# A new order for the first five units of a linear-attention stage, own-key weights by matrix products, and a bank moved

## The chip, the cores and the metric

The kernel runs on one core of one Trainium2 chip. The metric is the device time of one execution in microseconds: the median of three runs is 386.19 us (385.58 to 386.66). The engines are named as in the profile: PE (TensorE, matrix products), PEld (its weight loads), DVE (VectorE), ACT (ScalarE), POOL (GpSimd) and SP, which issues the DMAs. TensorE's granted clock is 1.00 at 2.4 GHz and 0.50 at 1.2 GHz.

## The reference

Three stages follow each other. The first is a linear attention with a decaying state, for 4 batches, 8 heads, 768 steps and head size 48:

```python
for t in range(S):
    kt, vt, rt = (k[:, :, t], v[:, :, t], r[:, :, t])
    cur = np.einsum('bhd,bhe->bhde', u[None] * kt, vt)
    y[:, :, t] = np.einsum('bhd,bhde->bhe', rt, state + cur)
    state = w[None, :, :, None] * state + np.einsum('bhd,bhe->bhde', kt, vt)
```

The weight of a step's own key is therefore sum over d of r * u * k, and that of an earlier step is r * k times a power of w. The second stage is a soft mixture of 8 experts with 4 slots each: logits x @ phi, one softmax over the 3072 tokens and one over the 32 slots, w1 (384 to 1024), a relu and w2 back. The third is a feed-forward layer: 384 to 2048, the square of the relu, 2048 to 384.

## The kernel before

A *unit* is a pair of heads of one batch: 16 units of 768 steps, cut into six chunks of 128 (three even, three odd). For a unit these steps are issued, each by a small function of its own:

- `load_unit`: one row per partition with r in its natural layout, r turned (heads by steps), k turned and v in its natural layout; 1344 KB, in five buffers. It is issued on SP's queue.
- `decay(n, m)`: DVE multiplies turned r (m = 0) or turned k (m = 1) by powers of w, held in a PSUM table `tabp` that DVE builds first.
- `turns(x, k)`: PE transposes unit k's keys back, in chunks of 48 columns, and, where x is given, the output of unit x. ACT copies both out.
- `A(n, par)`: PE forms the 128 by 128 score blocks of the even or odd chunks, in two tiles of the tag `ps("A")`, which has three banks.
- `pr1(n)`, `pr2(n)`, `weigh(n)`: POOL multiplies natural r by u and the inverse decay and then by the keys, and DVE sums over d. That gives `dg`, the own-key weights.
- `diag(n, par)`: POOL writes `dg` on the diagonal of an otherwise zero block `AT`. `cp(n, par)`: DVE copies the scores below the diagonal into it (copy_predicated, one instruction per head).
- `KV(n)`, `scan(n)`: PE forms the six chunk states, DVE runs the recurrence over them. `inter(n)` and `intra(n, par)`: PE forms the outputs from the states and from the blocks; ACT copies them out to `xT`. `L(n)`: PE adds the logits.

Each engine takes its instructions in the order in which the program issues them, and that order is written by hand: a prologue (L463 to L494) starts units 0 to 2, and a loop over n then interleaves unit n's last steps with the first ones of n+1, n+2 and n+3. After the last step of unit n the loop issues the load of unit n+5 and pieces of the expert weights. In the loop turn with n % 4 == 1 `both` (L389) transposes the exponentials and the logits of the batch that has just been finished, into the bank of tag `lg`, in which the next batch's logits will be summed; in turn 2 DVE also builds two small tables, `sel` and `rm` (L512, L514).

Ahead of the prologue `keep_clock(7)` issues seven products of the identity matrix with itself.

Of the kernel before, what the change touches and what calls it, by code (L numbers as in the profile page):

```python
# [17 lines left out]
def rwkv_softmoe_ffn(ctx: ExitStack, tc: tile.TileContext, un, k0, wt, u, phi, w1, w2, w_in, w_out, out):  # L18
    nc = tc.nc
    NU, NPC, _, PW = un.shape  # L20
    H, D = u.shape
    NP = H // 2
    B = NU // NP
    DM, NTOK = out.shape
    S = NTOK // B
# [5 lines left out]
    NS = phi.shape[1]  # L31
# [4 lines left out]
    NQ = 4  # L36

# [75 lines left out]
    k0n = kns[0]  # L113
    load_unit(0, (nc.sync, nc.sync, nc.sync))
    nc.scalar.dma_start(k0n.rearrange("p c h d -> p (c h d)"), k0)
    nc.scalar.dma_start(U0.rearrange("p b d -> p (b d)"),
                        u.rearrange("(a b) d -> a (b d)", b=2)[0:1].rearrange("a x -> (a x)").partition_broadcast(128))
    load_unit(1)
    phs = att.tile([112, NP, 2, NS], F32, name="phs")
    ident = const.tile([128, 128], F32, name="ident")  # L120
    make_identity(nc, ident)
    nc.gpsimd.memset(phs, 0.0)
    for hh in range(2):
        for par in range(2):
            nc.sync.dma_start(phs[64 * (hh ^ par):64 * (hh ^ par) + D, :, par],
                              phi.rearrange("(a b d) s -> b d a s", b=2, d=D)[hh])
# [79 lines left out]
    cur = pw[:, 0]  # L206
    nc.vector.memset(tabp[:, :, 64:65], 1.0)
    nc.vector.reciprocal(cur[:, :, 0], base[:, :NP])
    nc.vector.tensor_copy(cur[:, :, 1], base[:, :NP])
    nc.vector.tensor_copy(tabp[:, :, 63:64], cur[:, :, 0:1])  # L210
    for i in range(6):
        n = 1 << i
        blk = tabp[:, :, 64 - 2 * n:64 + 2 * n].rearrange("p a (q x) -> p a q x", q=4)
        nc.vector.tensor_tensor(blk[:, :, 0::3], blk[:, :, 1:3], cur.unsqueeze(3).to_broadcast([112, NP, 2, n]), ALU.mult)
        nxt_ = pw[:, (i + 1) % 2]
        nc.vector.tensor_mul(nxt_[:, :, 1], cur[:, :, 1], cur[:, :, 1])
        if i < 5:
            nc.vector.reciprocal(nxt_[:, :, 0], nxt_[:, :, 1])
        cur = nxt_

    def keep_clock(n):
        if n:
            p = ps("A")
        for _ in range(n):
            nc.tensor.matmul(p[:, :256], ident, ident.unsqueeze(1).to_broadcast([128, 2, 128]), start=True, stop=True)
# [20 lines left out]
    def turns(x, k):  # L246
# [142 lines left out]
    def both(b):  # L389
        p = ps("lg")[:, :384].rearrange("p (k h g) -> p k h g", k=2, h=2)  # L390
# [79 lines left out]
    nc.vector.tensor_tensor(rsc, tabp, uw.unsqueeze(2).to_broadcast([112, NP, 128]), ALU.mult)  # L470
    decay(0, 1, EV)
    decay(0, 0, EV)
    A(0, 0)
    decay(0, 1, OD)
    pp = ps("lg")
    for a in range(NP):
        nc.tensor.transpose(pp[:, a * 128:a * 128 + 112], rsc[:, a], ident[:112, :112])
    nc.scalar.copy(UT, heads(pp.rearrange("p (a e) -> p a e", a=NP)))  # L478
    turns(None, 0)
    weigh(0)  # L480
    diag(0, 0)
    decay(0, 0, OD)
    diag(0, 1)
    pr1(1)
    decay(1, 1)
    cp(0, 0)
    KV(0)
    turns(None, 1)
    pr2(1)
    decay(2, 1)  # L490
    scan(0)
    decay(1, 0)
    for x in xn:
        nc.gpsimd.memset(x[:, :, DM:DM + 1], 1.0)  # L494
# [3 lines left out]
    for _ in range(3):  # L498
        i, c = pieces.pop(0)
        load_weight(i, (c,))  # L500
    NL = NU - NB
    for j, pc in enumerate(pieces):
        loads[j * (NL + 3) // len(pieces)].append(pc)
    for n in range(NU):
# [5 lines left out]
        if n == 2:  # L510
# [56 lines left out]
        if n + NB < NU:  # L567
            load_unit(n + NB)
        for i, c in loads[n]:
            load_weight(i, (c,))  # L570
# [360 lines left out]
def _layout(r, k, v, w, u, w2):  # L931
# [15 lines left out]
    row = np.concatenate([nat(r), turned(r), turned(k), nat(v)], axis=2)  # L947
# [7 lines left out]
    return un, nat(k)[0], wt, u, w2p  # L955
# [27 lines left out]
```

## Time and profile before

| what | number |
|---|---|
| median of three runs | 386.19 us |
| the profiled execution's own time | 386.27 us |
| its span, first to last instruction | 384.5 us |
| PE busy | 370.6 us, 96% of the span |
| DVE busy | 270.2 us, 70% |
| ACT, POOL busy | 204.6 us, 104.8 us |
| mean granted TensorE clock | 0.978 |
| chain that ended last | PE 88%, DMA 4%, DVE 4% |

The profiled execution takes 1.8 us more than its span, and is 0.08 us above the median. PE's busy share hides that its first 28 us differ from the rest, so the profile is read by stretches: the attention stage ends at about 122 us, the experts at about 155 us, and the feed-forward layer fills the rest.

### The profile page before, as it was taken

How to read it: one execution, taken by the hardware profiler on the slowest of the kernel's cores; microseconds unless marked ns; L12 is line 12 of the kernel's file. 1: busy time of each engine (PE TensorE's matmuls, PEld its weight loads, DVE VectorE, ACT ScalarE, POOL GpSimd, SP SyncE). 2: the span in 40 equal slices, each digit the busy share in tenths (PEclk: the TensorE clock that was granted, in tenths of full speed). 3: DMA queues.
4: the chain of work that ended last, by engine and by line, in shares of the span. 5: the costliest groups of instructions: out<-in, count | busy, mean ns of one | idle time of the engine just before them, and what ended most of it. 6: DMA issues, size and time to landing. Idle time of an engine off the chain costs nothing.

```text
span 384.5 us, 8703 instructions
## 1 busy us (share of the span) xinstructions
PE 370.6 (96%) x3537; PEld 300.0 (78%) x3537; DVE 270.2 (70%) x470; ACT 204.6 (53%) x436; POOL 104.8 (27%) x115
## 2 busy tenths in 40 slices
PE   6799999999999999999999999999999999999996
PEld 4678988887878654788787888888888888888884
DVE  5669888989963387599886677566656675666563
ACT  2223444454444233599787866555555665555553
POOL 4566767777741322133222220000000000000000
PEclk9559999999999999999999999999999999999999
DMA  6979998998999999614242104000000030000004
GB/s 232 388 313 375 339 367 283 390 322 306 406 388 358 406 418 370 237 52 122 86 120 72 41 2 164 1 2 0 0 2 0 27 139 0 1 2 0 0 2 165
DMA packets 23176, 66.29 MB, mean 172 GB/s; under 512 B 3296, under 2 KB 4832, under 8 KB 23136
## 3 DMA queue, kind: packets, MB, share of 16 engines
q1 hardware_dynamic: 22848, 65.38, 45.7%
q8 instruction: 28, 0.46, 0.5%
q10 hardware_dynamic: 288, 0.34, 0.3%
q14 instruction: 12, 0.10, 0.1%
HBM read 60.21 MB, written 4.72 MB: 169 GB/s over the span
## 4 chain that ended last, share of the span: by engine, by line
PE 88%; DMA 4%; DVE 4%; ACT 2%; issue 1%; ACTq 0%; DVEq 0%
PE ps_A L915 26%; PE ps_Y L915 9%; PE ps_kv L915 9%; PE ps_lg L915 8%; PE ps_A L304 6%; PE ps_tr L820 6%; PE ps_YO L334 3%; PE ps_A L635 3%; PE ps_YE L343 3%; PE ps_Y L656 3%; PE ps_YO L343 3%; DMA slot<-in_un_dram 3%; PE ps_kv L316 2%; PE ps_lg L357 2%; DMA slot<-in_u_dram 2%; PE ps_YE L268 1%
## 5 line engine op out<-in xcount | busy, mean ns | idle before, releaser
L844 DVE TENSOR_TENSOR slot<-slot,slot 128x512 fp32r<-128x512 f32 (+1 forms) x97 | 71.8, 741 | 53.6 <-PE ps_kv L915 18.5
L915 PE MATMUL ps_A<-slot,slot 128*128 128x512 f32 x432 | 105.8, 389 | 0.0
L915 PEld LDWEIGHTS ps_A<-slot,slot 128*128 128x128 f32 x432 | 81.0, 188 | 17.1 <-ACT slot L841 0.3
L841 ACT CAST slot<-slot 128x512 fp32r<-128x512 f32 (+1 forms) x97 | 59.7, 616 | 49.5 <-DVE slot L838 49.2
L831 ACT ACTIVATE slot<-ps_tr 128x512 f32<-128x512 f32 (+1 forms) x97 | 57.4, 593 | 23.2 <-PE ps_tr L820 22.3
L838 DVE TENSOR_TENSOR slot<-slot 128x512 f32<-128x512 f32 (+1 forms) x71 | 48.4, 684 | 11.5 <-ACT slot L831 11.2
L915 PE MATMUL ps_Y<-slot,slot 128*128 128x512 f32 x144 | 55.4, 391 | 0.0
L915 PE MATMUL ps_kv<-slot,slot 128*128 128x512 f32 x144 | 55.1, 389 | 0.0
L915 PE MATMUL ps_lg<-slot,slot 128*128 128x512 f32 x144 | 55.0, 389 | 0.0
L309 DVE COPY_PREDICATED AT<-mask,ps_A 128x384 f32<-128x384 int32 x64 | 34.0, 586 | 12.3 <-PE ps_A L304 4.2
L304 PE MATMUL ps_A<-slot 48*128 48x128 f32 x384 | 35.2, 303 | 4.6 <-DVE slot L235 3.2
L820 PE MATMUL ps_tr<-slot,slot 128*128 128x512 f32 x96 | 37.4, 391 | 0.4 <-DVE slot L784 0.4
L304 PEld LDWEIGHTS ps_A<-slot 48*128 48x128 f32 x384 | 29.0, 201 | 9.1 <-DVE slot L235 3.7
L294 POOL TENSOR_SCALAR_AFFINE_SELECT AT<-dg 128x768 f32<-128x768 f32 x32 | 28.2, 884 | 26.2 <-PE ps_YE L343 19.4
L235 DVE TENSOR_TENSOR slot<-slot,ps_tab 112x768 f32<-112x768 f32 (+1 forms) x34 | 30.1, 891 | 5.1 <-DMA slot<-in_un_dram 5.1
L700 POOL TENSOR_TENSOR slot<-wf,slot 128x384 fp32r<-128x384 f32 x16 | 18.2, 1136 | 55.6 <-ACT slot L695 55.6
L915 PEld LDWEIGHTS ps_Y<-slot,slot 128*128 128x128 f32 x144 | 27.0, 188 | 5.9 <-issue 0.4
L915 PEld LDWEIGHTS ps_kv<-slot,slot 128*128 128x128 f32 x144 | 27.0, 188 | 5.7
L915 PEld LDWEIGHTS ps_lg<-slot,slot 128*128 128x128 f32 x144 | 27.0, 188 | 5.5
L346 ACT COPY xT<-ps_YE 112x384 f32<-112x384 f32 x16 | 7.7, 478 | 38.7 <-PE ps_YE L343 38.7
L283 POOL TENSOR_TENSOR slot<-slot,slot 128x576 f32<-128x576 f32 x16 | 22.7, 1417 | 9.2 <-ACT slot L275 8.9
L279 POOL TENSOR_TENSOR slot<-slot,slot 128x576 f32<-128x576 f32 x15 | 21.3, 1420 | 0.4 <-ACT slot L478 0.4
(202 smaller groups left out, 527.8 us busy)
## 6 DMA issues: line engine op xcount, KB each, us to landing
slot<-in_un_dram SPq DMA_DIRECT2D x15, 1344.0 KB, 6.8
slot<-in_w_dram SPq DMA_DIRECT2D x24, 512.0 KB, 8.3
slot<-in_w_dram SPq DMA_DIRECT2D x8, 1536.0 KB, 10.3
slot<-in_w_in_dram SPq DMA_DIRECT2D x4, 1536.0 KB, 8.8
wo<-in_w_out_dram SPq DMA_DIRECT2D x16, 384.0 KB, 3.4
out_dram<-slot SPq DMA_DIRECT2D x18, 256.0 KB, 2.1
slot<-in_un_dram SPq DMA_DIRECT2D x3, 448.0 KB, 6.8
slot<-slot SPq DMA_DIRECT2D x48, 16.0 KB, 1.8
```

Source lines behind the costliest of these rows:

```text
L235: nc.vector.tensor_tensor(x, x, t.unsqueeze(1).to_broadcast(list(x.shape)), ALU.mult)
L283: nc.gpsimd.tensor_tensor(rv, rv, st[n, "kn"] if by is None else by, ALU.mult)
L294: nc.gpsimd.affine_select(out=at, in_=dg.unsqueeze(3).to_broadcast([128, 2, HC, 128]), pattern=[[0, 2], [0, HC], [1, 128]], compare_op=ALU ...
L304: nc.tensor.matmul(p[h][:, i], tv[rows, 1, 2 * i + par], tv[rows, 0, 2 * i + par], start=True, stop=True)
L309: nc.vector.copy_predicated(st[n, "AT", par][:, h], mask.unsqueeze(1).to_broadcast([128, HC, 128]), p)
L343: nc.tensor.matmul(p[o:o + D, i], vv[:, 2 * i + par, h], at[:, h, i], start=False, stop=True, skip_group_check=True)
L820: nc.tensor.matmul(p, gst[:, 128 * f:128 * (f + 1)], cTall[:, 512 * g:512 * (g + 1)], start=True, stop=True)
L831: nc.scalar.activation(fs[i, "hr"][:, c], fs[i, "p"][:, c], AF.Relu)
L838: nc.vector.tensor_mul(gg, hr, hr)
L841: nc.scalar.copy(part(i, "gh")[:, c], fs[i, "gg"][:, c])
L844: nc.vector.tensor_tensor(part(i, "gl")[:, c], fs[i, "gg"][:, c], fs[i, "gh"].bitcast(F32)[:, c], ALU.subtract)
L915: nc.tensor.matmul(o, (hi, lo, hi)[k][:, 128 * j:128 * (j + 1)], (gh, gh, gl)[k], start=(f == 0 and k == 0), stop=(f == NF - 1 and k == 2))
```

## The change

The rows of a unit are laid out anew (turned k, turned r, v, natural r), and a second array, `ph`, holds phi in the form in which the kernel needs it, made on the host as a layout. Units 0 to 2 are loaded in three pieces each and without natural r; unit 3 in three pieces; the separate loads of unit 0's natural k, of u and the four loads of phi are gone, and phi comes as one load after unit 1.

For units 0 to 2 `pr1`, `pr2` and `weigh` are replaced: POOL (for half of unit 0, DVE) multiplies the decayed r and k, in which the powers of w cancel (`rk`), and PE sums over d with u as the two moving columns (`dg_of`): 24 products of 32 by 2 for a unit, and one ACT copy.

The prologue now issues everything that comes ahead of loop turn 4, and the loop starts there (`N0 = 4`). It holds twelve `filler` products of the identity matrix; `both` uses a bank of tag A; `sel` and `rm` are built in turn 7; the table of powers is built from all squares first and one reciprocal; the key transposes of units without an x use the `kv` bank twice instead of a bank of tag A.

```diff
-        return units[n % NB][:112, ON:ON + OT].rearrange("p (m c t) -> p m c t", m=2, c=NC)
+        return units[n % NB][:112, :OT].rearrange("p (m c t) -> p m c t", m=2, c=NC)[:, ::-1]
...
+        if n > R:
+            nc.sync.dma_start(dst, un[n].rearrange("q p f -> p q f"))
         else:
             for q in range(NPC):
-                engs[q].dma_start(dst[:, q], un[n, q])
+                w = PW if n == R else min(PW, OT + ON - q * PW)
+                nc.sync.dma_start(dst[:, q, :w], un[n, q, :, :w])
...
+    def filler(n):
+        for _ in range(n):
+            nc.tensor.matmul(pp[:, 384:512], ident, ident, start=True, stop=True)
...
-            rest = [kvp[:, NC * D:NC * D + 2 * D], kvp[:, NC * D:NC * D + 2 * D] if x is not None else ps("A")[:, :2 * D]]
+            rest = [kvp[:, NC * D:NC * D + 2 * D]] * 2
...
     def both(b):
-        p = ps("lg")[:, :384].rearrange("p (k h g) -> p k h g", k=2, h=2)
+        p = ps("A")[:, :384].rearrange("p (k h g) -> p k h g", k=2, h=2)
...
+    def rk(n, cs=slice(0, NC), eng=nc.gpsimd):
+        tv = t_view(n)
+        eng.tensor_tensor(rk_view(n)[:, cs], tv[:, 0, cs], tv[:, 1, cs], ALU.mult)
+
+    def dg_of(n):
+        o = kvp[:, NC * D + 2 * D:NC * (D + 2) + 2 * D].rearrange("p (c h) -> p c h", h=2)
+        x = rk_view(n)
+        for c in range(NC):
+            for g in range(4):
+                nc.tensor.matmul(o[32 * g:32 * g + 32, c], x[:, c, 32 * g:32 * g + 32], uw2[:, n], start=True, stop=True)
+        st[n, "dg"] = wk([128, 2, NC], "dg", 2)
+        nc.scalar.copy(st[n, "dg"].rearrange("p h c -> p c h"), o)
...
+    N0 = 4
...
+    decay(0, 1, OD)
+    decay(0, 1, EV)
+    turns(None, 0)
+    decay(0, 0, OD)
+    A(0, 1)
+    decay(0, 0, EV)
+    rk(0, EV)
+    carry_of()
+    KV(0)
...
+    turns(0, 3)
+    decay(4, 1)
+    pr2(3)
+    A(2, 0)
+    A(2, 1)
+    cp(2, 0)
+    inter(2)
...
-    for n in range(NU):
+    for n in range(N0, NU):
...
-        if n == 2:
+        if n == 7:
```

PE's order at the start of the program, before; `slot_1_71` and `slot_2_72` hold units 0 and 1, L304 is A(0, 0), L477 the transposes of the inverse decay, L268 `turns` and L316 `KV` (rows that only repeat these are left out):

```order
L225 MATMUL ps_A_147<-ident 128x256 x7
L304 MATMUL ps_A_164<-slot_1_71 128x128
L304 MATMUL ps_A_165<-slot_1_71 128x128
L477 MATMUL ps_lg_173<-ident,xT_157 128x112 x4
L268 MATMUL ps_kv_115<-ident,slot_1_71 128x48
L268 MATMUL ps_YO_117<-ident,slot_1_71 128x48
L268 MATMUL ps_YE_116<-ident,slot_1_71 128x48
L268 MATMUL ps_A_179<-ident,slot_1_71 128x48
L316 MATMUL ps_kv_115<-slot_1_71,slot_15_85 48x48 x10
```

The same stretch of PE now; L269 is `turns`, L306 A(0, 1), L318 `KV`, L481 `dg_of` and L226 `filler`:

```order
L222 MATMUL ps_lg_147<-ident 128x256 x7
L269 MATMUL ps_kv_115<-ident,slot_1_71 128x48
L269 MATMUL ps_YO_117<-ident,slot_1_71 128x48
L269 MATMUL ps_YE_116<-ident,slot_1_71 128x48
L306 MATMUL ps_A_177<-slot_1_71 128x128
L306 MATMUL ps_lg_147<-slot_1_71 128x128
L318 MATMUL ps_kv_115<-slot_1_71,slot_15_85 48x48 x10
L481 MATMUL ps_kv_115<-slot_14_84,slot_1_71 32x2 x24
L226 MATMUL ps_lg_147<-ident 128x128 x12
```

The key transposes, which need turned k alone, have come ahead of the scores, which need r too; the transposes of the inverse decay have gone to a later place, and 24 small products and 12 fillers stand ahead of unit 1's keys.

DVE's order from the end of the table on, before; L470 scales the table by u, L235 is `decay`, L287 `weigh`, L309 `cp`:

```order
L470 TENSOR_TENSOR xT_157<-ps_tab_122,slot_14_84 112x512
L235 TENSOR_TENSOR slot_1_71<-slot_1_71,ps_tab_122 112x3x128 x3
L287 TENSOR_REDUCE dg_196<-slot_1_71 128x12
L235 TENSOR_TENSOR slot_1_71<-slot_1_71,ps_tab_122 112x3x128
L235 TENSOR_TENSOR slot_2_72<-slot_2_72,ps_tab_122 112x768
L309 COPY_PREDICATED AT_198<-mask,ps_A_164 128x384
L309 COPY_PREDICATED AT_198<-mask,ps_A_165 128x384
L235 TENSOR_TENSOR slot_3_73<-slot_3_73,ps_tab_122 112x768
```

The same stretch of DVE now; L211 is the table's last product, L236 `decay`, L474 `rk` for half of unit 0, L322 `scan(0)`, L486 the scaling by u, L311 `cp`:

```order
L211 TENSOR_TENSOR ps_tab_122<-ps_tab_122,slot_14_84 112x4x2x32
L236 TENSOR_TENSOR slot_1_71<-slot_1_71,ps_tab_122 112x3x128 x4
L474 TENSOR_TENSOR slot_1_71<-slot_1_71 112x3x128
L236 TENSOR_TENSOR slot_2_72<-slot_2_72,ps_tab_122 112x768 x2
L322 SCALAR_TENSOR_TENSOR slot_15_85<-ps_kv_115,slot_15_85 112x288
L486 TENSOR_TENSOR slot_13_83<-ps_tab_122,slot_14_84 112x512
L311 COPY_PREDICATED AT_241<-mask,ps_A_177 128x384
L311 COPY_PREDICATED AT_241<-mask,ps_lg_147 128x384
L311 COPY_PREDICATED AT_226<-mask,ps_A_262 128x384
```

All four decays of unit 0 and both of unit 1 now stand ahead of the first masked copy, and no sum over d is left among them.

## Rows read from the trace of the kernel before

**Rows 1.** The page's part 1: busy time and share of the span by engine.
```profile
PE 370.6 (96%) x3537; PEld 300.0 (78%) x3537; DVE 270.2 (70%) x470; ACT 204.6 (53%) x436; POOL 104.8 (27%) x115
```

**Rows 2.** Busy time by stretch: us, engines' busy us (instructions), granted clock, DMA share, GB/s.
```profile
1.50:7.40 5.90, 5.90 (x14) 4.47 (x14) 4.54 (x26) 1.95 (x3) 1.27 (x6) 1.00 0.71 221
7.60:10.60 3.00, 0.00 (x0) 0.00 (x0) 0.95 (x3) 0.33 (x1) 2.75 (x2) 0.99 1.03 421
10.80:20.40 9.60, 7.68 (x84) 6.47 (x84) 6.61 (x11) 3.05 (x13) 5.97 (x8) 0.50 1.05 388
21.00:27.50 6.50, 6.50 (x78) 5.51 (x77) 4.40 (x7) 0.48 (x1) 2.83 (x4) 0.50 0.84 341
28.00:120.00 92.00, 89.85 (x1808) 76.09 (x1809) 77.43 (x131) 40.95 (x132) 62.88 (x61) 1.00 0.93 349
```

**Rows 3.** Timeline of the first 18 us: start, us, instruction, idle before and releaser.
```profile
1.43 6.08 PE L225 MATMUL ps_A<-ident 128*128 128x256 f32 x14 [1.43 <-POOL ident masks.py:199]
...
6.21 0.43 DVE L214 TENSOR_TENSOR ps_tab<-ps_tab,slot 112x256 f32<-112x256 f32 x1
...
9.65 1.48 DVE L235 TENSOR_TENSOR slot<-slot,ps_tab 112x384 f32<-112x384 f32 x3 [2.14 <-DMA slot<-in_un_dram]
...
10.72 1.66 PE L304 MATMUL ps_A<-slot 48*128 48x128 f32 x12 [3.22 <-DVE slot L235]
...
12.31 1.01 PE L477 MATMUL ps_lg<-ident,xT 112*128 112x112 f32 x4
...
13.41 0.95 DVE L235 TENSOR_TENSOR slot<-slot,ps_tab 112x768 f32<-112x768 f32 x1 [1.16 <-DMA slot<-in_un_dram]
...
17.18 0.95 DVE L235 TENSOR_TENSOR slot<-slot,ps_tab 112x768 f32<-112x768 f32 x1 [1.83 <-DMA slot<-in_un_dram]
```

**Rows 4.** Start of the chain that ended last: start, us, what.
```profile
1.25 6.16 DMA slot<-in_u_dram
7.42 9.73 DMA slot<-in_un_dram
```

**Rows 5.** Busy time of two early stretches, columns as in rows 2.
```profile
3.00:6.00 3.00, 3.00 (x9) 2.37 (x8) 2.49 (x18) 0.22 (x2) 0.00 (x0) 1.00 0.69 182
7.00:10.00 3.00, 0.51 (x2) 0.04 (x1) 0.86 (x2) 0.93 (x1) 2.37 (x2) 1.00 1.03 419
```

**Rows 6.** The same chain at the high clock, one loop turn, columns as in rows 4.
```profile
28.42 0.04 PE ps_kv L268
...
29.21 0.88 PE ps_A L304 x11
30.09 0.57 PE ps_lg L357 x12
30.66 0.28 PE ps_YO L334 x2
...
31.49 0.58 PE ps_kv L316 x20
32.08 0.66 PE ps_YE L343 x12
```

**Rows 7.** Timeline of the same turn, DVE and POOL, columns as in rows 3.
```profile
28.51 1.07 DVE L309 COPY_PREDICATED AT<-mask,ps_A 128x384 f32<-128x384 int32 x2 [2.07 <-issue]
...
29.47 0.94 DVE L235 TENSOR_TENSOR slot<-slot,ps_tab 112x768 f32<-112x768 f32 x1
...
30.69 1.42 POOL L283 TENSOR_TENSOR slot<-slot,slot 128x576 f32<-128x576 f32 x1 [1.34 <-ACT slot L275]
```

**Rows 8.** Busy time of loop turns 2, 3 and 5, columns as in rows 2.
```profile
33.39:39.95 6.56, 6.12 (x127) 5.27 (x126) 6.56 (x11) 2.49 (x8) 4.57 (x6) 1.00 1.03 396
39.95:45.78 5.83, 5.83 (x127) 5.18 (x126) 5.08 (x9) 2.49 (x8) 4.50 (x5) 1.00 0.84 294
...
51.63:58.59 6.96, 6.58 (x130) 5.51 (x130) 5.78 (x10) 3.26 (x11) 4.51 (x5) 1.00 0.93 347
```

**Rows 9.** PE's waits from 28 to 128 us: total us, times, longest.
```profile
PE ps_lg L357 <- ACT nat L395: 1.1, 3, 0.4
```

More of the change, by code (lines that the diff above doesn't have):

```diff
@@ L213, in rwkv_softmoe_ffn @@
         blk = tabp[:, :, 64 - 2 * n:64 + 2 * n].rearrange("p a (q x) -> p a q x", q=4)
[L214 to L219, printed above, removed]
+        by = pw[:, :, i].rearrange("p s a -> p a s").unsqueeze(3).to_broadcast([112, NP, 2, n])
+        nc.vector.tensor_tensor(blk[:, :, 0::3], blk[:, :, 1:3], by, ALU.mult)
+    nc.gpsimd.tensor_tensor(uw, base[:, :NP], base[:, NP:], ALU.mult)
+    nc.gpsimd.memset(uw2, 0.0)
+    for h in range(2):
+        rows = slice(64 * h, 64 * h + D)
+        nc.gpsimd.tensor_copy(uw2[rows, :, h:h + 1], uw[rows, :R].unsqueeze(2))
+    for i in (5, 6):
+        nc.gpsimd.tensor_tensor(pos[:, i + 1], pos[:, i], pos[:, i], ALU.mult)
     def keep_clock(n):
[L222 to L223 removed]
         for _ in range(n):
[L225 removed]
+            nc.tensor.matmul(pp[:, :256], ident, ident.unsqueeze(1).to_broadcast([128, 2, 128]), start=True, stop=True)
+    def filler(n):
+        for _ in range(n):
+            nc.tensor.matmul(pp[:, 384:512], ident, ident, start=True, stop=True)
     def idle(n, m, cols):
@@ L299, in A @@
         tv = t_view(n)
-        p = [ps("A")[:, :HC * 128].rearrange("p (c t) -> p c t", c=HC) for _ in range(2)]
+        p = [ps("A"), ps("A") if n or not par else pp]
+        p = [x[:, :HC * 128].rearrange("p (c t) -> p c t", c=HC) for x in p]
         for i in range(HC):
@@ L470, in rwkv_softmoe_ffn @@
[L470 to L494, printed above, removed]
+    rsc = early[NSLOT - 1][:112, :NP * 128].rearrange("p (a t) -> p a t", a=NP)
+    def rk_view(n):
+        return units[n][:112, OT + ON:OT + ON + NC * 128].rearrange("p (c t) -> p c t", c=NC)
+    def rk(n, cs=slice(0, NC), eng=nc.gpsimd):
+        tv = t_view(n)
+        eng.tensor_tensor(rk_view(n)[:, cs], tv[:, 0, cs], tv[:, 1, cs], ALU.mult)
@@ L496, in rwkv_softmoe_ffn, with UT_of, carry_of @@
+    def UT_of():
+        for a in range(NP):
+            nc.tensor.transpose(pp[:, a * 128:a * 128 + 112], rsc[:, a], ident[:112, :112])
+        nc.scalar.copy(UT, heads(pp.rearrange("p (a e) -> p a e", a=NP)))
+    def carry_of():
+        nc.gpsimd.tensor_copy(carry[:, :, :, 1:], pos[:, 7].unsqueeze(2).unsqueeze(3).to_broadcast([112, NP, D, NC - 1]))
+        for x in xn:
+            nc.gpsimd.memset(x[:, :, DM:DM + 1], 1.0)
     loads = [[] for n in range(NU)]
     pieces = [(i, c) for i in range(NEARLY) for c in range(3)]
-    for _ in range(3):
-        i, c = pieces.pop(0)
-        load_weight(i, (c,))
@@ L501, in rwkv_softmoe_ffn, with load_next @@
-    NL = NU - NB
-    for j, pc in enumerate(pieces):
-        loads[j * (NL + 3) // len(pieces)].append(pc)
-    for n in range(NU):
+    NL = NU - NB
+    for j, pc in enumerate(pieces[3:]):
+        loads[j * (NL + 3) // (len(pieces) - 3)].append(pc)
+    def load_next(n):
+        if n + NB < NU:
+            load_unit(n + NB)
+        for i, c in loads[n]:
+            load_weight(i, (c,))
+    N0 = 4
+    for i, c in pieces[:3]:
+        load_weight(i, (c,))
+    decay(0, 1, OD)
+    decay(0, 1, EV)
@@ new lines, in rwkv_softmoe_ffn @@
+    turns(None, 0)
[5 more added lines that the diff above has]
+    KV(0)
+    rk(0, OD, nc.vector)
+    dg_of(0)
+    diag(0, 0)
+    decay(1, 1)
+    decay(1, 0)
+    filler(2)
+    scan(0)
+    filler(2)
+    filler(2)
+    filler(2)
+    filler(2)
+    diag(0, 1)
+    filler(2)
+    rsc_of()
+    turns(None, 1)
+    A(0, 0)
+    inter(0)
+    cp(0, 1)
+    cp(0, 0)
+    rk(1)
+    dg_of(1)
+    diag(1, 0)
+    decay(2, 0)
+    intra(0, 0)
+    decay(2, 1)
@@ new lines, in rwkv_softmoe_ffn @@
+    diag(1, 1)
+    KV(1)
+    scan(1)
+    intra(0, 1)
+    rk(2)
+    UT_of()
+    A(1, 1)
+    turns(None, 2)
+    A(1, 0)
+    cp(1, 1)
+    inter(1)
+    load_next(0)
+    dg_of(2)
+    pr1(3)
+    diag(2, 1)
+    diag(2, 0)
+    decay(3, 1)
+    cp(1, 0)
+    decay(4, 0)
+    decay(3, 0)
+    intra(1, 0)
+    pr1(4)
+    KV(2)
+    intra(1, 1)
+    scan(2)
+    load_next(1)
+    L(0)
+    turns(0, 3)
[5 more added lines that the diff above has]
+    inter(2)
+    cp(2, 1)
@@ new lines, in rwkv_softmoe_ffn @@
+    weigh(3)
+    diag(3, 0)
+    intra(2, 0)
+    pr1(5)
+    KV(3)
+    scan(3)
+    intra(2, 1)
+    load_next(2)
+    decay(5, 1)
+    L(1)
+    turns(1, 4)
+    A(3, 0)
+    A(3, 1)
+    turns(2, 5)
+    A(4, 0)
+    diag(3, 1)
+    L(2)
+    cp(3, 0)
+    inter(3)
+    pr2(4)
+    intra(3, 0)
+    decay(5, 0)
+    cp(3, 1)
+    KV(4)
+    weigh(4)
+    intra(3, 1)
+    load_next(3)
+    decay(6, 1)
+    diag(4, 0)
+    pr2(5)
+    cp(4, 0)
+    diag(4, 1)
+    scan(4)
+    for n in range(N0, NU):
@@ L566, in rwkv_softmoe_ffn @@
             soft4(prev)
[L567 to L570, printed above, removed]
+        load_next(n)
         if n + NB >= NU:
```

68 lines of the change are left out of this document (31 added, 37 removed).

## The prediction

> **What bounds the kernel now.** I read the page's shares first: PE is busy for 96% of the span [rows 1], so only two things can shorten the time: less work on PE, or a better use of its first microseconds. The table by stretches shows the second one. From 28 to 120 us PE is busy 89.85 of 92 us at a granted clock of 1.00, the level of 2.4 GHz. From 10.8 to 27.5 us it runs at 0.50, 1.2 GHz, and in the first 9.6 us of that it is idle a fifth of the time [rows 2]. The timeline says why. The seven identity products end at 1.43 + 6.08 = 7.51 us; PE then has nothing to do until 10.72, because DVE waits for unit 0's load until 9.65 [rows 3]. In this idle stretch the clock falls [rows 2]. Units 1 and 2 land 3.8 us apart, at 13.41 and 17.18, and DVE waits for each [rows 3]; the chain that ended last starts with the load of u and then a unit's load [rows 4]. So the start is bound by loads, and after it by PE at half its clock.
>
> The point at which both kernels stand in the same state is the start of loop turn 4: A(4, 0), scan(4) and intra(3, 1) are done. Before, it is at 45.78 us [rows 8]. What the change gains by then is carried to the end, if the rest only moves.
>
> **The start.** The table of powers is done at 6.21 + 0.43 = 6.64 us before [rows 3]; the new order of its small steps I count as nothing. When does unit 0's turned k land? It is now the first piece, 448 KB, with nothing but w's table ahead of it, where 288 KB of natural k and u's slow load shared the queues. Upper bound: 9.65, when all three pieces had landed [rows 3]. Lower bound: it cannot help before the table, 6.6. At even the poor rate of the early stretch, 182 GB/s [rows 5], 448 KB need 2.5 us, and the first load is issued at about 1.3 us; I take 6.6. The turned r follows 2.5 us later at that rate, or 1.1 us at 419 GB/s [rows 5], and A(0, 1) wants it near 8 us. Then two half decays (1.48 / 3 = 0.49 us each [rows 3]) let PE begin the key transposes at about 7.6, right behind the identity products: the idle stretch of 3.2 us goes, and with it, I expect, the fall of the clock.
>
> **PE's work from 7.5 us to the start of turn 4, at the high clock.** Durations are those of one turn at that clock [rows 6]:
> nine A of 0.88: 7.9; three `turns` with output of 0.79 (28.42 to 29.21): 2.4; three with keys alone, half of that plus the ACT copy of about a quarter that now stands between the two uses of the kv bank, 0.65: 2.0; four `inter` of 0.83 (30.66 to 31.49): 3.3; five `KV` of 0.58: 2.9; eight `intra` of 0.66: 5.3; three `L` of 0.57: 1.7; the transposes of the inverse decay, half of 1.01 [rows 3]: 0.5. That is 26.0 us that both kernels have to do.
> Added are the own-key products: each of the 24 is two instructions, as `KV`'s ten are 20, and those 20 take 0.58, so 29 ns each; 3 x 48 x 29 ns = 4.2 us. The trace has no product with two columns. Bounds: no gain is possible, since the instructions were not there (0 below), and 47 ns, what one of `L`'s twelve takes with 128 columns [rows 6], or 6.8 us, above. I take `KV`'s price because its products are the nearest in size. Added too are twelve fillers: 128 columns in two instructions, of which one `intra` does six rounds in 0.66, so 12 x 0.22 = 2.6 us. In all 32.8 us.
>
> The Trainium skill, "TensorE: Matmul & The Clock Gate", section "Wait — 56ns, not 53.3ns?", gives about 62 ns for a matmul where the sequencer's microcode decodes it, and 25 ns start to start as the floor otherwise. `KV`'s 29 ns in this trace stand near the floor, not near 62. By the 62 ns the added products would cost 8.9 us instead of 4.2.
>
> **Waits that remain on PE.** A(2, 0) and A(2, 1) now stand back to back, as do A(3, 0) and A(3, 1), with A(4, 0) close behind. Four tiles want three banks, so the second A waits for the first masked copy of the first A, half of 1.07 us [rows 7], plus hand-overs: 0.65, 0.65 and 0.3, so 1.6. What is queued behind them is PE's own next work, inter and intra, so all of it is paid. DVE's work in the stretch is 2.0 for unit 0's half decays, 11 whole decays of 0.94 and 9 pairs of masked copies of 1.07 [rows 7], and ten instructions under 1 us: about 29 us from 6.6 on, 35.6, so it ends ahead of PE and the three sums over d that it loses are worth nothing by themselves. POOL's `rk` takes 1.42 x 768 / 576 = 1.9 us [rows 7] and stands ahead of `dg_of` of units 1 and 2; unit 0's fillers and scores, and for unit 2 the transposes and A of unit 1, cover it. If they did not, PE would wait there for the rest.
> 7.5 + 32.8 + 1.6 = 41.9, against 45.78: **3.9 us earlier**.
>
> **The loop.** Turn 2 takes 6.56 us against 5.83 for turn 3, with DVE busy for all 6.56, since it builds `sel` and `rm` there [rows 8]. Now turn 7 pays it: 0.7 back. PE waits 1.1 us in three turns for ACT's copy out of the lg bank [rows 9]; with the transposes in a bank of A the wait goes, 1.1 less. A's next tiles then come one bank later and could wait up to half a copy pair, 0.5 us in each of three turns; turn 5 with its 6.96 us and DVE busy for 5.78 [rows 8] has room for it, so I count 1.0 as gained. Net 0.3 less.
> The loads: natural r of three units, natural k and u, 3 x 288 + 288 + 48 = 1200 KB, fall away, 2.9 us at 419 GB/s. A unit's load is issued behind the last step of the unit five earlier and moves with it, so the 93% of the DMA engines [rows 2] do not hold the gain back.
>
> Sum: 3.9 + 0.3 = 4.2 earlier. Of that I take back 0.5 for hand-overs between engines in the new prologue that a sum of durations does not hold; PE's idle fifth from 10.8 to 20.4 [rows 2] says such things are there. 386.27 - 3.7 = 382.6; the median shown is 0.08 below the profiled execution, so **382.5 us**. The bounds of the small products (4.2 us less, 2.6 more) do not lie evenly: near zero is ruled out by `KV`, so I use 1 less and 2 more. With up to 1 us of the waits, the forecast's own range is 380.8 to 384.6.
>
> **Rivals.**
> *B, the clock falls for a short while.* The new start is a run of short products (transposes of 48 columns, 20 and 48 small ones), and before the clock did not come back in 9.6 us of such work at 80% busy nor at once in 6.5 us at 100% [rows 2]. Against it: the same mix at 98% busy has held 1.00 for 92 us [rows 2], and PE has no gap over 0.2 us here. A takes 1.66 us at the low level against 0.88 [rows 3, 6], a factor of 1.9. If PE is low from about 10.6 to 16 us and the fillers bring it back, 5.4 us do the work of 2.9: 2.5 more, 385.0.
> The Trainium skill, "TensorE: Matmul & The Clock Gate", section "Part 1: The HAM clock gate", says that the chip's activity window runs free and does not restart with the kernel. By that the point of a fall or rise would differ between executions, and the median could lie between the forecast and B; one trace cannot show it.
> *C, slower: the clock falls and stays low as it did before, which lasted 17 us.* Place: PE, from about 10.6 to 24 us, until the dense `intra` products of unit 1. 13.4 us then do the work of 7.1: 6.3 more, 388.8, since fillers and small products, which the old kernel did not have, are paid at the low level too. It turns slower from some 8 us at the low level on, 8 x 0.47 = 3.7. For it: before, the level came back only at the end of 6.5 fully busy microseconds [rows 2]. A late first piece would bring it about, since an idle PE is what let the clock fall.
> *D, the small products cost `L`'s 47 ns or more.* 3 x 48 x 18 ns = 2.6 more: 385.1. Against it stands `KV`. By the 62 ns of the Trainium skill's page named above it would be 387.2.
> *E, it does not arrive.* The expert weights keep the end of the attention stage where it was: 386. Against it: the loads move along and are 1.2 MB fewer.
>
> **Chances.** Forecast 0.60, B 0.17, C 0.13, D 0.06, E 0.04. A measurement of this kernel tells about 0.3%, 1.16 us, from no change: faster is below 385.0. Faster: 0.60, half of B and half of D, 0.71. Same: half of B, E and a third of D, 0.15. Slower: C and the rest of D, 0.14. The range from 380.7 to 386.8 leaves out C and the lower end of the forecast.
>
> **What would show it.** Right: PE's key transposes start by 8 us, no idle stretch over 1 us on PE from 7.5 us on, granted clock 1.00 from 7.5 to 42, A(4, 1) at about 42, `dg_of` at about 1.4 us for a unit, PE without a wait for L395's successor, and turn 7 some 0.7 us longer than its neighbours. Wrong: a row at 0.50 between 8 and 28 us (B or C by its length), DVE waiting for unit 0 beyond 7 us, or `dg_of` beyond 2 us. The sum fails as a whole if A(4, 1) comes earlier and the end does not.

## The result and the profile after

The changed kernel takes **380.31 us** (median of 4, 379.74 to 380.59) against 386.43 (385.58 to 386.97) on the same chip: a ratio of 0.984, with a 95% interval of 0.982 to 0.986. It is 6.1 us faster; 3.7 were forecast. The direction held, and so did the mechanism of the start; one term of the sum was mis-sized, and the time lies 0.5 us under the range. Its profiled execution took 380.17 us with a span of 378.5.

The same stretches as in [rows 2], where the key transposes now begin at 7.05:

```profile
1.50:7.05 5.55, 5.05 (x15) 3.83 (x16) 4.86 (x20) 0.79 (x2) 1.91 (x11) 1.00 0.84 259
7.05:28.00 20.95, 20.00 (x464) 17.58 (x464) 16.16 (x25) 7.24 (x26) 14.65 (x15) 1.00 1.03 408
28.00:120.00 92.00, 90.37 (x1795) 76.38 (x1795) 73.91 (x131) 41.14 (x130) 58.09 (x57) 1.00 0.93 352
```

PE is busy for 20.0 of the 20.95 us to 28, and the granted clock is 1.00 (2.4 GHz) where [rows 2] have 0.50. The timeline of the first 9 us, for DVE and PE, answers to [rows 3]:

```profile
4.25 1.69 DVE L211 TENSOR_TENSOR ps_tab<-ps_tab,slot 112x8 f32<-112x8 f32 x6
5.98 1.95 DVE L236 TENSOR_TENSOR slot<-slot,ps_tab 112x384 f32<-112x384 f32 x4
...
8.79 0.95 DVE L236 TENSOR_TENSOR slot<-slot,ps_tab 112x768 f32<-112x768 f32 x1 [0.40 <-DMA slot<-in_un_dram]
```

```profile
1.44 5.12 PE L222 MATMUL ps_lg<-ident 128*128 128x256 f32 x14 [1.44 <-POOL ident masks.py:199]
7.05 0.26 PE L269 MATMUL ps_kv<-ident,slot 48*128 48x48 f32 x1 [0.50 <-DVE slot L236]
```

The powers are ready at 5.94, unit 0's turned k has landed by then (at 4.52), and PE stands still for 0.50 us where it had stood 3.22. So the table of powers, and no longer the load of unit 0, now sets when PE starts. The chain that ended last, in the stretch that the prediction priced (columns as in [rows 4]; in this and the chains below, pieces under 0.1 us are left out):

```profile
9.39 0.51 PE ps_kv L481 x46
9.90 2.88 PE ps_lg L226 x24
12.78 0.19 PE ps_kv L269
...
13.06 0.25 ACT slot L266
13.36 0.26 PE ps_kv L269
13.68 0.74 PE ps_A L306 x12
...
25.50 0.81 PE ps_A L306 x12
26.34 0.59 DVE AT L311
26.97 1.19 PE ps_A L306 x10
...
39.86 0.87 PE ps_A L306 x12
```

L481 is `dg_of`, the own-key products: 0.51 us on the chain for the 48 matmul instructions of a unit, so 11 ns each. L226 are the fillers, L269 to L269 a turn with keys alone and ACT's copy in its middle, and 26.34 is the wait of A(2, 1) for the masked copy. Turn 4, A(4, 1), starts at **39.86** against 45.78 before. Turns 4, 5 and 7 answer to [rows 8], PE's waits from 28 to 128 us to [rows 9]:

```profile
39.86:45.70 5.84, 5.84 (x126) 5.19 (x126) 5.74 (x11) 2.64 (x9) 4.21 (x5) 1.00 0.83 295
45.70:52.23 6.53, 6.50 (x130) 5.51 (x130) 5.57 (x10) 3.27 (x11) 4.48 (x5) 1.00 0.92 325
59.38:65.53 6.15, 6.11 (x126) 5.27 (x126) 6.15 (x11) 2.49 (x8) 5.00 (x7) 1.00 0.82 290
```

```profile
PE ps_A L306 <- DVE AT L311: 0.5, 1, 0.5
PE ps_kv L702 <- DVE m L697: 0.4, 1, 0.4
...
```

Turn 5 takes 6.53 us against 6.96, and the logits no longer wait for ACT's copy. Turn 7 takes 6.15, since it builds `sel` and `rm`. Of the 6.9 us that the loop hands on, 0.9 goes again in this execution: 0.4 in the last output's landing (3.5 us behind the last copy against 3.1), and 0.5 in the middle of the last stage, where ACT waits for an output that lands late:

```profile
303.52 0.37 ACT L1031 COPY slot<-ps_kv 128x256 f32<-128x256 f32 x1 [1.99 <-DMA out_dram<-slot]
```

### The profile page after: what moved, and what is told of

It is laid out like the page before. It is cut to its first block, busy times and chain, and to the rows that moved or that the text cites. A ratio compares the mean times of both kernels' runs of the same rounds, so it can differ in the third digit from the quotient of the medians.

```text
span 378.5 us, 9041 instructions
## 1 busy us (share of the span) xinstructions
PE 368.8 (97%) x3705; PEld 298.6 (79%) x3705; DVE 266.6 (70%) x460; ACT 203.9 (54%) x438; POOL 106.6 (28%) x118
## 3 DMA queue, kind: packets, MB, share of 16 engines
q1 hardware_dynamic: 22240, 64.52, 45.2%
## 4 chain that ended last, share of the span: by engine, by line
PE 91%; DVE 5%; DMA 2%; ACT 1%; issue 1%; ACTq 0%; DVEq 0%
PE ps_A L1023 25%; PE ps_Y L1023 9%; PE ps_kv L1023 8%; PE ps_lg L1023 8%; PE ps_A L306 7%; PE ps_tr L928 6%; PE ps_YO L336 3%; PE ps_A L743 3%; PE ps_YE L345 3%; PE ps_Y L764 3%; PE ps_YO L345 3%; PE ps_kv L318 2%; PE ps_lg L359 2%; DVE AT L311 1%; DMA out_dram<-slot 1%; PE ps_YE L269 1%
## 5 line engine op out<-in xcount | busy, mean ns | idle before, releaser
L952 DVE TENSOR_TENSOR slot<-slot,slot 128x512 fp32r<-128x512 f32 (+1 forms) x97 | 69.5, 718 | 53.3 <-ACT slot L949 18.5
L311 DVE COPY_PREDICATED AT<-mask,ps_A 128x384 f32<-128x384 int32 x63 | 33.6, 586 | 12.9 <-PE ps_A L306 7.9
L808 POOL TENSOR_TENSOR slot<-wf,slot 128x384 fp32r<-128x384 f32 x16 | 22.3, 1394 | 51.6 <-ACT slot L803 51.6
L306 PE MATMUL ps_A<-slot 48*128 48x128 f32 x378 | 33.3, 289 | 1.2 <-DVE AT L311 1.0
L306 PEld LDWEIGHTS ps_A<-slot 48*128 48x128 f32 x378 | 27.3, 188 | 5.2 <-DVE AT L311 2.2
L236 DVE TENSOR_TENSOR slot<-slot,ps_tab 112x768 f32<-112x768 f32 (+1 forms) x34 | 29.9, 891 | 1.0 <-DMA slot<-in_un_dram 1.0
L928 PEld LDWEIGHTS ps_tr<-slot,slot 128*128 128x128 f32 x96 | 17.9, 188 | 4.2 <-DVE slot L892 0.6
L284 POOL TENSOR_TENSOR slot<-slot,slot 128x576 f32<-128x576 f32 x13 | 18.4, 1417 | 7.4 <-ACT slot L276 7.1
```

Of the source, the lines that this page charges most:

```text
L236: nc.vector.tensor_tensor(x, x, t.unsqueeze(1).to_broadcast(list(x.shape)), ALU.mult)
L311: nc.vector.copy_predicated(st[n, "AT", par][:, h], mask.unsqueeze(1).to_broadcast([128, HC, 128]), p)
L808: nc.gpsimd.tensor_tensor(wout_half(wls, f, 5), st.pop(("wf", f)), hi, ALU.subtract)
L928: nc.tensor.matmul(p, gst[:, 128 * f:128 * (f + 1)], cTall[:, 512 * g:512 * (g + 1)], start=True, stop=True)
L952: nc.vector.tensor_tensor(part(i, "gl")[:, c], fs[i, "gg"][:, c], fs[i, "gh"].bitcast(F32)[:, c], ALU.subtract)
```

## The experiments

The theory after reading the two traces: PE is at the high clock from the start on (this is what the new order and the fillers buy), and the small products cost 11 ns an instruction, not the 29 that I took from `KV`. Rivals: the clock alone would have done it; the fillers are dead weight; the products cost more than their rows show. "Before" is 385.9 to 386.2 us in the runs below.

**e1: no fillers.**
```diff
-        for _ in range(n):
+        for _ in range(0):
             nc.tensor.matmul(pp[:, 384:512], ident, ident, start=True, stop=True)
```


> The changed kernel without its twelve fillers. Theory 1 (the clock is held by the real work alone, and the fillers stand on PE's path): granted clock 1.00 throughout, turn 4 starts about 1.1 us earlier than the 39.86 us of the changed kernel, time about 379.2 us. Theory 2 (the fillers hold the clock): a row at 0.50 appears between 10 and 24 us, turn 4 starts at 40.5 to 43 us, time 381 to 383.5 us. Theory 3 (another engine would wait anyway, the fillers stand in idle time): the same time as the changed kernel within 0.3 us.

382.24 us (ratio 0.991, 0.988 to 0.993), so the fillers earn 1.9 us.

```profile
10.00:12.00 2.00, 0.82 (x53) 0.66 (x41) 2.00 (x3) 0.28 (x2) 1.59 (x5) 1.00 1.01 381
...
14.00:31.00 17.00, 16.84 (x274) 14.42 (x274) 9.11 (x13) 3.92 (x12) 8.20 (x8) 0.50 0.92 358
```

PE is idle for over half of 10 to 12 us, and the clock is down from 14 to 31. This profiled execution took 385.5 us at a mean clock of 0.976; the others, at 0.985 to 0.991, took 381.3 to 382.7. One and the same program spends differently long at the low level.

**e3: no identity products at the start** (`keep_clock(7)` to `keep_clock(0)`).


> The changed kernel without the seven identity products ahead of its first work, so that PE starts at the low level at about 6.7 us. Theory 1 (what the order gains, it gains mostly through the clock): low until the fillers have run, turn 4 starts at 43 to 44 us, time 383.5 to 384.5 us. Rival (the loads and the order are the gain, the clock matters little there): turn 4 at 40 to 41 us, time 380.5 to 381.5 us.

383.86 us (0.994, 0.993 to 0.995). The products run at the low level from the start: `dg_of` of unit 0 and the fillers take

```profile
10.58 0.82 PE L481 MATMUL ps_kv<-slot,slot 112*32 112x2 f32 x48
11.33 5.07 PE L226 MATMUL ps_lg<-ident 128*128 128x128 f32 x22
```

where 24 filler instructions took 2.88. Turn 4 starts at 43.8. (The record names the clock only from its first change on, so here the durations tell it.)

**e4: the kernel before, with 15 identity products instead of 7.**


> The old kernel with 15 identity products instead of 7, so that PE is busy until unit 0 has landed; nothing else is changed. Theory 1 (the lost clock is the larger part of what the change won): granted clock 1.00 from about 7 us on, turn 1 starts at about 23.3 us instead of 27.5, time 382 us. Rival (the loads bind the start, so a fast PE waits for units 1 and 2): turn 1 at 26.5 us or later, time 385.5 us or more. In between, the difference to 380.3 is what loads, order and own-key products win by themselves.

385.4 us (0.998, 0.997 to 1.000). The clock stays up until 16 us and is at the low level from 15.9 to 26.2 us, where PE still waits for units 1 and 2 (it is busy for 1.4 of the 2 us from 14 to 16). So in the old order a high clock up to 16 us is worth 0.6 us by that ratio. A high clock throughout, without the new loads and order, no run has.

**e5: the transposes of the exponentials back in the logits' bank** (`ps("A")` to `ps("lg")` in `both`).


> The changed kernel with one part undone: the transposes of the exponentials stand in the logits' bank again. Theory (the bank gives what turns 5, 9 and 13 show, 6.53 us against 6.96 before, 0.44 x 3 = 1.3 us): 381.6 us, PE waits again for ACT's copy at the first L of those turns, turn 4 still starts at about 39.9. Rival (A's next tiles now find their bank earlier, so the wait only changes its place): 380.3, within 0.3 of the changed kernel.

381.13 us, 0.8 more than the changed kernel. PE's waits from 28 to 128 us:

```profile
PE ps_lg L359 <- ACT nat L397: 1.1, 3, 0.4
PE ps_A L306 <- DVE AT L311: 0.5, 1, 0.5
```

The old wait is back, and the start of turn 15 lies 1.28 us further behind that of turn 4 than in the changed kernel, 3 x 0.43. At the end only 0.8 is left, since this kernel does not lose the 0.5 us behind the late output. **e15** does the same edit alone in the kernel before, the other way round:


> One part of the change alone: the kernel before, with the transposes of the exponentials in a bank of the score products. Theory (each of turns 5, 9 and 13 gets 0.43 us shorter, as they do between the two kernels): 1.3 us earlier, 385.0 us. Rival (the bank helps only beside the new order of the start): 386.3.

384.6 us (0.9965, 0.995 to 0.998; 12 runs): 1.4 less. So the bank gives 1.3 to 1.4 us, with the new start or without.

**e6: no own-key products for units 1 and 2.**
```diff
-        for c in range(NC):
+        for c in range(NC if n == 0 else 0):
```


> Leaves out part of the computation: the 48 small own-key product instructions of units 1 and 2 (unit 0's stay; the copy by ACT and POOL's products before them stay). Theory (11 ns each as the rows of the changed kernel show, so 2 x 0.51 us): 1.0 us earlier, 379.3 us. Rival (they hold PE for the 29 ns each that the prediction took, the rest of it not seen in the rows): 2 x 1.4 = 2.8 us earlier, 377.5. Second rival (without them PE only waits longer for the masked copies): within 0.3 of 380.3.

379.47 us, 0.84 less; but turn 4 starts only 0.20 earlier. The chain shows what took the products' place:

```profile
18.23 0.87 PE ps_A L306 x12
19.21 1.05 DVE AT L311 x2
20.26 0.83 DVE slot L236
21.09 0.52 DVE AT L311
```

From 19 to 21.6 us DVE is the bound then. Most of the rest of the 0.84 is again the 0.5 us of the late output, which this kernel does not pay. So at turn 4 only a fifth of the theory's 1.0 us arrives, the rest lies beside waits for DVE's work, and the second rival comes nearest. The 2.8 us of the first rival are nowhere.

**e2: the own-key products issued twice.**
```diff
+        for c in range(NC):
+            for g in range(4):
+                nc.tensor.matmul(o[32 * g:32 * g + 32, c], x[:, c, 32 * g:32 * g + 32], uw2[:, n], start=True, stop=True)
```


> The changed kernel with every own-key product of units 0 to 2 issued twice (the second pass writes the same numbers): 3 x 48 more instructions. Theory 1 (such a product costs what the trace of the changed kernel shows, 48 in 0.51 us, 11 ns each): 3 x 0.51 = 1.5 us more, or less where a wait covers it, 381.2 to 381.8 us. Theory 2 (the price of KV's, 29 ns, as the prediction had it): 4.2 us more, 384.5 us.

389.54 us (1.008, 1.005 to 1.011), far more than any price per product. Neither theory foresaw the chain:

```profile
15.64 0.49 PE ps_kv L481 x46
...
16.15 0.40 PE ps_kv L484 x29
...
17.34 0.44 PE ps_kv L318 x19
17.78 3.80 issue
21.58 0.31 PE ps_kv L318
```

The second set (L484) costs 0.40 us. Then, in the middle of `KV(1)`, PE stands for 3.80 us with no releaser and everything it needs in place. The clock falls within that stop, at 19.5 us. What does PE lack there? The queue named "instruction" moves one packet of 16 KB in 18 to 20 us. The page of the changed kernel has its packets, MB and share, and beside PE's its instructions:

```profile
PE 368.8 (97%) x3705; PEld 298.6 (79%) x3705; DVE 266.6 (70%) x460; ACT 203.9 (54%) x438; POOL 106.6 (28%) x118
...
q8 instruction: 29, 0.48, 0.5%
```

That is 29 packets for 2 x 3705 matmuls and weight loads of PE. The kernel before has 28 for 2 x 3537, and e2 has 30 for 2 x 3849: each time one for 253 to 257 of PE's instructions. So these are PE's instructions.

**e7: e2, with 1.5 MB of expert weights loaded later.**


> As the run with the own-key products issued twice, but the first three pieces of expert weights (1.5 MB) are loaded some 10 us later, so that the DMA queues are idle for a while around 17 us. Theory I (PE's stop of 3.80 us in the middle of KV(1) is a wait for its next packet of instructions, which stands behind the data that keep the queues busy): the stop shrinks to under 1 us, the clock does not fall, 381.8 us, which is the changed kernel and 3 x 0.45 us. Theory II (the stop comes from the doubled products themselves, whatever the queues do): again 3.5 to 4 us at the same instruction, about 389.

389.96 us (1.010, 1.008 to 1.012); the stop is 3.09 us, so the time of theory I is missed. But the run did not do what it was made for. The DMA share (the figure before the last) shows full queues ahead of the stop and quiet ones only within it:

```profile
16.00:18.00 2.00, 2.00 (x126) 1.95 (x126) 2.00 (x3) 0.32 (x2) 0.67 (x1) 1.00 1.03 423
18.00:21.00 3.00, 0.25 (x11) 0.13 (x5) 0.01 (x1) 0.34 (x1) 2.79 (x3) 0.98 0.28 112
```

The data run out at about 18.3 us, and the packet moves at 19.10. So this run leaves theory I open. What it does show is the count of records up to the stop, the same in e2 and in e7, though one reaches it 0.5 us later:

```profile
0.00:17.78 17.78, 15.88 (x349) 13.54 (x349) 13.67 (x33) 4.08 (x13) 9.38 (x26) 1.00 0.89 326
```

```profile
0.00:18.25 18.25, 16.54 (x349) 13.99 (x349) 13.75 (x33) 4.08 (x13) 9.37 (x26) 1.00 0.89 324
```

349 matmuls and 349 weight loads, **698** records. Both stops end some 2.3 us after the packet starts to move (19.21 us in e2, 19.10 in e7).

**e9: the products twice in unit 2 alone** (the added loop of e2 with `range(NC if n == 2 else 0)`).


> The changed kernel with the 24 own-key products issued twice for unit 2 alone. Theory (the small products cost about 9 ns for each added instruction, as the doubled ones of units 0 and 1 showed with 0.42 us for 48; PE's long stop in the runs with all of them doubled comes where PE has used up its loaded instructions, after some 698 matmul and weight-load records, before the next packet of 16 KB is in at about 21.4 us): at unit 2 that packet is in, so there is no stop over 0.5 us, and turn 4 starts 0.45 us later, 380.75 us. Rival I (doubled products themselves bring a stop of 3 to 4 us behind them): 384 to 388. Rival II (29 ns each, as the prediction priced them): 1.4 us more, 381.7.

386.04 us: the time that rival I gave, and my theory's 380.75 missed. The stop is there, elsewhere:

```profile
22.80 0.38 PE ps_kv L484 x36
...
25.08 0.55 PE ps_lg L359 x9
25.63 3.05 issue
28.68 0.64 PE ps_lg L359 x3
```

```profile
0.00:25.63 25.63, 22.67 (x475) 19.22 (x476) 20.01 (x43) 7.18 (x22) 15.32 (x31) 1.00 0.93 335
```

It stands at record 475 + 476 = 951, 253 behind the 698 of e2, and comes 2.45 us after the last doubled product. These views leave out PE's semaphore instructions; with them the two stops stand at 705 and 961, exactly 256 apart. In the traces of all runs but e13, PE has 14 stops of over 0.07 us without a releaser between 8 and 122 us, and each of them stands at record 705 or a multiple of 256 away from it. So PE uses up a packet, and the next one is not there: I had the mechanism, and overlooked that the next boundary follows. In the runs with stops PE passes record 442 at 15.3 (e2) and 15.8 (e7) and record 698 at 22.4 (e9), and gets past the boundary after that 6.3, 5.6 and 6.3 us later. The changed kernel passes 442, 698 and 951 at 15.6, 21.7 and 27.7: it is served just in time, with no spare.

The traces also bear on theory I of e7. In the changed kernel the DMA engines are full around the first five boundaries, from 9.6 to 34.4 us, and each packet moves 3.4 to 3.9 us after PE has passed the boundary. At five later ones, at 40.6, 46.8, 59.9, 72.4 and 85.4 us, the engines carry data for less than a fifth of the half microsecond before. There the packet moves 2.2 us after PE in the first case, and in the other four 0.2 to 0.8 us before PE gets to the boundary. At the other eight up to 122 us, with the engines mostly full again, it moves 0.3 to 3.1 us after PE. This speaks for a packet that waits behind data, but does not settle it; no run has tested it.

The Trainium skill, "Runtime: NRT & Kernel Launch", section "Instruction fetch mechanics", says that instructions come in blocks of 16 KiB, 256 instructions each, and that crossing a boundary is mostly hidden. The size agrees with the 256 records here. That it is hidden does not: the stops measure 3.05 to 3.80 us where short products use up a block faster than the next one comes.

**e13: the same time, few instructions.** Behind each `dg_of` of units 0 to 2 stands
```diff
+    filler(2)
```


> The control for the runs with own-key products issued twice: behind the products of units 0, 1 and 2 stands each time the PE time that the doubling added (0.4 to 0.5 us), but as four identity instructions in place of 48 small ones. Theory (PE stops where it has used up its loaded instructions: the stops stood at records 698 and 951, 253 apart, and ended 2.3 us after a packet of 16 KB had moved): no stop over 0.5 us without a releaser, the clock holds, 1.0 to 1.4 us more than the changed kernel, 381.3 to 381.7 us. Rival (0.45 us more at these places is what upsets the prologue, by whatever kind of instruction): a stop of 3 us or the clock at 0.50 again, 386 to 389.

Three executions took 381.61, 381.65 and 383.48 us. The one with the trace took 2047.76 us, with PE busy from end to end, so that its waits cannot be read; why is open. **e16** is the same kernel once more:


> The kernel of the control once more, for a trace: the profiled execution of the first was one in which PE ran at a fraction of its rate from the first instruction to the last (2046 us), so that its waits can't be read; its timed ones gave 381.61, 383.48 and 381.65. Theory (supply of instructions): 381.6 us, no stop without a releaser over 0.5 us, the clock at 1.00 from 8 to 40 us. Rival (the added time itself): a stop near 18 or 26 us, 386 or more.

383.57 us (0.992, 0.990 to 0.995; 381.45 to 384.89). At a mean clock of 0.999 or 1.000 it took 381.45 to 382.21; at 0.988 to 0.996, 383.6 to 384.9. The profiled one is of the last kind. PE's only wait without a releaser up to 128 us:

```profile
PE ps_A L306 <- issue: 0.4, 1, 0.4
```

That one ends at 28.12, where record 951 passes. The long stop is gone, so it came from the number of instructions and not from the time. But the clock part of my expectation missed: from 29.7 to 36.5 us this execution was at the low level.

**e10: own-key products 128 columns wide.**
```diff
-            for g in range(4):
-                nc.tensor.matmul(o[32 * g:32 * g + 32, c], x[:, c, 32 * g:32 * g + 32], uw2[:, n], start=True, stop=True)
+            nc.tensor.matmul(o[:, c], x[:, c], uw2[:, n], start=True, stop=True)
```


> The changed kernel with 6 own-key products of 128 weight columns a unit in place of 24 of 32: 12 instructions instead of 48. Theory (four products of 32 columns run beside one another in the array, so the price goes by instructions of full width, 60 to 110 ns each by the identity and filler rows): 0.7 to 1.3 us a unit against 0.51, 380.9 to 382.7 us in all. Rival (the price goes by the count of instructions, 11 ns each): 0.13 us a unit, 379.2 us.

382.34 us (12 runs): at a clock of 0.997 or more, 382.04 to 382.42; the other five, at 0.978 to 0.993, 383.98 to 390.04. The chain gives each `dg_of`

```profile
9.39 1.43 PE ps_kv L480 x12
```

119 ns for each instruction of 128 weight columns. The same columns in four instructions of 32 take 4 x 11 = 43 ns. In the trace of the changed kernel the narrow ones start in groups of four, 7 ns apart, with a new group every 32 ns, though each lasts 171 ns; the wide ones start 112 ns apart. So the narrow ones, each in its own quarter of the columns, run beside one another, and no price of a full-width product carries over to them.

**e12: units 0 to 2 loaded whole** (`w = PW`), 864 KB more ahead of the rest.


> The changed kernel, but units 0 to 2 are loaded whole again, with the natural r that nothing there reads: 3 x 288 KB more in the first queue. Theory (the start is bound by loads; the changed kernel's DVE waits 0.4 us for unit 1): unit 1's turned pieces land 0.7 us later and unit 2's 1.5 to 2.2 us later; the first delay lies in the fillers' cover, the second in unit 1's work, 380.3 to 381.5 us. Rival (every microsecond of load delay comes out at the end, and the clock falls as PE waits): 383 or more.

383.73 us, from 380.81 to 385.94: 380.8 to 381.5 at a clock of 0.997 or more, 383.1 to 385.9 below. The delay itself costs about 1 us, as the theory had it, and in six of the ten executions the clock falls on top, as the rival had it. Its trace also has three stops of some 0.3 us without a releaser, at records 442, 698 and 951.

**e8: 7 fillers, and the first score products of units 2 and 3 one step earlier.**
```diff
+    A(2, 0)
+    cp(2, 0)
     L(0)
     turns(0, 3)
     decay(4, 1)
     pr2(3)
-    A(2, 0)
     A(2, 1)
-    cp(2, 0)
```
(and the same for unit 3.)


> The changed kernel with 7 fillers instead of 12, and with the first score products of units 2 and 3 one step earlier (before the logits and the transposes), so that the two halves no longer stand back to back. Theory: the key transposes of unit 1 are ready at about 11.5, so 1.0 us of the fillers is plain cost, and the two waits for the masked copies, 0.52 us each, go: 2.1 us earlier, 378.2 us, at a granted clock of 1.00. Rival (fewer fillers let the clock fall, as none did): 381 to 382.5 with a stretch at 0.50. Second rival (the fillers covered a wait that now shows, only the score products' 1.0 us is gained): 379.3.

**379.15 us** (378.92 to 381.11; 0.984, 0.982 to 0.986), 1.2 less; the traced execution holds the clock at 1.00. The run changes two things at once, so it does not price the five fillers by themselves. Two things ate part of the 2.1: PE then waits for ACT's output copies (0.5 and 0.7 us), and at 21.26 there is a stop in the middle of `dg_of(2)`, at the packet's end again:

```profile
20.90 0.36 PE ps_kv L481 x32
21.26 0.19 issue
21.45 0.31 PE ps_kv L481 x16
```

**e11: e8 with the logits behind the second score products, and the wide own-key products.**


> The run with 7 fillers and the score products apart, with two edits more: the logits stand between the second score products and the products that wait for ACT's output copies, and the own-key products are 128 columns wide (fewer instructions). Theory: the ACT waits of 0.5 and 0.7 us in front of the inter products of units 2 and 3 go in part, and the 0.2 us stop of PE without a releaser at 21.26 goes because fewer instructions are used up by then: 378.0 to 378.6 us. Rival (wide products cost what they save, and the ACT waits only move): 379.2 to 380.

381.28 us, outside what either theory gave: the wide products cost 0.9 us a unit more, and the clock is at 0.50 from 24 to 27.5 us. **e14** is the same with the narrow products:
```diff
     A(2, 0)
     cp(2, 0)
-    L(0)
     turns(0, 3)
...
     A(2, 1)
+    L(0)
```


> The run with 7 fillers and the score products apart (379.15 us), with the logits between the second score products and the products that wait for ACT's output copies, and the own-key products 32 columns wide as in the changed kernel. Theory (ACT's copies held PE for 0.5 us at 26 and again at 33 us, and 0.57 us of logits cover them): 0.5 to 1.0 us earlier, 378.2 to 378.7. Rival (PE's instructions come in no faster: record 951 can't pass before about 27.5 us, 6 us after record 698, whatever the order): 379.1, with a new stop without a releaser of 0.2 to 0.6 us near 27 us.

**378.48 us** (378.15 to 379.40; 0.982, 0.980 to 0.984), the best of all and 1.8 below the changed kernel. The theory's range is hit. Of the rival's stop at record 951 only 0.1 us shows, at 27.0; a stop of 0.4 us stands at 45.2, again at the end of a packet.

## Why the prediction fell short

- **What bounds the kernel now; the start.** Right. PE's key transposes begin at 7.05 (7.6 said), the idle stretch is 0.5 us, and no row stands at 0.50. The half microsecond comes from the table of powers, which is done at 5.94 instead of 6.64; its new order was counted as nothing. e3 and e4 show both halves: without the high clock at the start the new order loses 3.6 us, and a high clock up to 16 us in the old order gives 0.6.
- **PE's work from 7.5 us: the step that failed is the term for the own-key products.** It said 3 x 48 x 29 ns = 4.2 us; the rows show 3 x 0.51 = 1.5. `KV`'s price was taken because "its products are the nearest in size". Any other product of before would have been a wrong neighbour too: four products of 32 columns run beside one another (e10), which no row of before shows. The bound below, zero, was cut to "1 less" with `KV` as the reason, and just there the truth lay, 2.7 less. Had I kept the bound, the range would have held the time. (The parts named for the range add up to 380.5 to 385.5, a little wider than the 380.8 to 384.6 stated; the time lies under both.) The Trainium skill, "TensorE: Matmul & The Clock Gate", section "Wait — 56ns, not 53.3ns?", gives some 25 ns start to start as the floor; an estimate by it would be 3.6 us. The rows decide for 11 ns.
- Smaller terms of that sum: the start 0.45 earlier; fillers 2.9 (2.6 said); turns with keys alone 0.75 to 0.9 each (0.65 said, 0.6 too little in all); waits of A(2, 1) and A(3, 1) 0.66 each with their hand-overs, 1.3 in all (1.6 said, with a third that does not show). These and the rest take back 0.7 of the 2.7; turn 4 came at 39.86, 2.0 before the 41.9.
- **The loop.** Turns 5, 9 and 13 give 1.3 (1.0 said), and turn 7 pays 0.3 instead of 0.7. Net 1.0 where 0.3 stood. DVE is busy for all 6.15 us of turn 7, as it was for all 6.56 of turn 2 [rows 8]: it has 0.4 less to do beside the two tables.
- **The 0.5 taken back for hand-overs** was not needed in the prologue. By luck, 0.9 went at the end, for which I had no term, and brought the time nearer to the forecast.
- **Rivals.** B and C did not happen, but what they rest on is real: e1 has the low clock for 17 us, and e12 and e16 fall into it in some executions. D is refuted by the rows, E by turn 4, which came earlier and took the end with it.
- What nobody priced: the added instructions themselves. The changed kernel shows no stop, as record 698 passes when its packet is in; only A(2, 1), within which record 951 falls, takes 1.19 us where the other score blocks on the chain take 0.74 to 1.05. The products of one unit issued once more, 48 matmuls and 48 weight loads, turn the gain into the old time (e9).

Open: whether the data in front of PE's packet make up the 5.6 to 6.3 us from one boundary to the packet for the next, as the traces suggest; and why the clock falls in some executions of e12 and e16 and not in others. Some kernels wait 2 us for an output in the last stage and some don't; I did not follow that.

## What to carry to other kernels

A product with few columns in a part of the array has no price in the rows of full-width ones: measure it, or keep its lower bound at zero in the range. Count instructions as well as microseconds where products are short, since here, with the DMA engines full, PE's next 256 came some 6 us after the last boundary, and a stop of 3 us there took the clock down with it. Fillers are worth their time where they cover a wait: 12 beat none by 1.9 us, and in e8, 7 of them with the scores apart were better still.

## What the runs showed of the hardware

- 48 instructions of 32 weight columns and 2 moving columns take 0.51 us (11 ns each); 12 of 128 weight columns take 1.43 (119 ns each).
- PE stops for 3.05 to 3.80 us at matmul and weight-load records 698 and 951, 256 apart with the semaphore instructions, with nothing else to wait for; all 14 stops of PE without a releaser stand at such multiples.
- The time of one and the same program goes by how long its clock is low: e16 takes 381.45 us at a mean clock of 1.000 and 384.89 at 0.989, e12 380.81 at 0.997 and 385.94 at 0.986.
